# P·V banks as two tiles, and the third score tile given back behind attention for two one-bank tiles

## The chip, the cores and the metric

The kernel runs on one core of a Trainium2 chip. Times are device microseconds (us) of that core. A run's time is the span from the first to the last instruction, plus 1.8 us around it in the profiled execution.

The core has TensorE (PE, with its weight loads shown as PEld), VectorE (DVE), ScalarE (ACT), GpSimd (POOL), and SyncE (SP), which issues the transfers. PE's products go to PSUM, which this kernel uses as eight banks of 128 partitions by 512 fp32 words.

## What is computed

Three layers, all in fp32 values:

```
scores = (mean of neighbouring query pairs) @ k.T / sqrt(64)     # 4 x 8 heads, 576 x 1152
x = softmax(scores) @ v                                          # 2304 tokens x 512
h = x @ w_in ; g = where(h > 0, h, exp(min(h, 0)) - 1)           # 2304 x 2048
x = g @ w_out                                                    # 2304 x 512
logits = x @ phi                                                 # 2304 x 32 slots
d = softmax over tokens ; slots = d.T @ x                        # 32 x 512
slot_out = relu(slots @ w1[e]) @ w2[e]                           # 8 experts
out = softmax over slots(logits) @ slot_out                      # 2304 x 512
```

## The kernel before

**Stages.** Attention runs over 16 pairs of heads. Each pair has 18 steps: two halves `h` of the query columns times nine chunks `c` of 128 keys. A step forms scores of both heads in a score tile (L664), ACT takes the exponential (L676), POOL or DVE adds it to a running sum (L685), and PE multiplies it with V (L671). P·V of half 0 accumulates in PSUM bank `psC[0]`, that of half 1 in `psC[1]`. At the end of a half, ACT copies the result out (L500, the helper of all copies), PE forms the column sums in the same bank (L695) and ACT takes them (L698).

The next pair's keys are prepared during the last steps of a half. PE transposes them (L580), two thirds into a score tile, one third into `psC[1]`, while half 0 of the pair before still accumulates in `psC[0]`. ACT makes the rounded copy (L587), DVE the remainder (L588). Row maxima go through `psC[h]` too (L642, L649).

The dense layer runs over 32 slots (8 groups of weights for three batches together, then 8 for the last). The hidden product (L817) goes to tile `psA`; ACT and DVE apply the ELU (L828 to L831) and split it into two rounded parts (L500, L503). The output product (L856) comes in groups of six products: column half `t = 0` in `psC[0]`, `t = 1` in `psC[1]`. DVE adds each group to X (L867). As each batch ends, the slot layer's first part runs between these groups: logits (L875, L881), transposes (L1019, L969), slot sums (L1023), and weights of the slots (L1042). Its PSUM is `psB[0]` and `psB[1]`, the two banks of the third score tile. The experts (L1180, L1208) read 32 MB of weights, and the last products (L1239) alternate between `psA` and `psB` and are scaled by ACT (L1244) or DVE (L1246).

**PSUM tiles.** There are four tiles of two banks each. `psA` has two; the third of `psT` serves scores during attention (`psS = psT`), and its two halves are `psB`. `psC` is two halves of one tile:

```
psT = [psum.tile([P, 2, 512], F32, name=f"psA{i}") for i in range(3)]
psCt = psum.tile([P, 2, 512], F32, name="psC")
psB = [psT[2][:, i] for i in range(2)]
psC = [psCt[:, i] for i in range(2)]
```

**Order.** `Plan` sets the order. Every operation is recorded with a planned time, its engines, its duration, and what it reads and writes; the plan orders them by a list schedule with engine costs, and emits them by planned start. In the plan's own book, the banks are separate names (`("C", 0)`, `("C", 1)`, `B` in places 4 and 5). The waits between engines are not written by the plan. The layer that holds the tiles adds them when an instruction is emitted, from the tiles that it touches. Each engine runs its queue in order, so a waiting instruction holds what is queued behind it.

Of the kernel before, what the change touches and what calls it, by code (L numbers as in the profile page):

```python
# [8 lines left out]
F32 = mybir.dt.float32  # L9
# [6 lines left out]
PSUM = bass.MemoryType.PSUM  # L16
# [14 lines left out]
def dve(n):  # L31
    return n / 960 + 0.145
# [18 lines left out]
class Plan:  # L51
# [11 lines left out]
    def add(self, t, eng, dur, fn, r=(), w=(), size=0.0, mode="F", port=False, fixed=False):  # L63
        if isinstance(eng, str):
            eng, dur = (eng,), (dur,)
        cls = (self.tag or str(self.phase)) + "".join(x.rstrip("0123456789") for x in w[0][:2] if isinstance(x, str)) + (eng[0] if len(eng) == 1 else "*")
        self.ops.append([t, len(self.ops), eng, dur, fn, r, w, size, BIAS[3 if self.tag else self.phase], t + PRI.get(cls, 0.0), cls, mode, port, fixed])
# [214 lines left out]
def attention_moe_softmoe(  # L282
# [12 lines left out]
    nc = tc.nc  # L295
    P = 128
    B, H, S, D = q.shape
# [4 lines left out]
    NP = B * H // 2  # L302
# [3 lines left out]
    KD = DM // P  # L306
# [7 lines left out]
    PAIR = 2 * NC * STEP  # L314
# [5 lines left out]
    plan = Plan(LOOK)  # L320
    add = plan.add
# [3 lines left out]
    psum = ctx.enter_context(tc.tile_pool(name="psum", bufs=1, space=PSUM))  # L325
# [7 lines left out]
    phi_sb = const.tile([P, KD, 2, NS], F32, name="phi_sb")  # L333
    wscr = dram.tile([2, NG, P, KD * GF * P], F32, name="wscr")
    rscr = [dram.tile([2 * NC, D], F32, name=f"rscr{i}") for i in range(2)]
    psT = [psum.tile([P, 2, 512], F32, name=f"psA{i}") for i in range(3)]
    psCt = psum.tile([P, 2, 512], F32, name="psC")
    psA, psS = psT[:2], psT
    psB = [psT[2][:, i] for i in range(2)]
    psC = [psCt[:, i] for i in range(2)]  # L340
    plan.rot.update(A=[(0, 1), (2, 3)], B=[(4,), (5,)], S=[(0, 1), (2, 3), (4, 5)])
    for name, cnt in (("E", 3), ("U", 3), ("H", 5), ("L", 5)):
        plan.rot[name] = [(f"{name}{i}",) for i in range(cnt)]
# [26 lines left out]
    def carve(kind, name, n, size, off=None, first=0, late=False):  # L370
        lo = top[kind] if off is None else off
        res = []
        for i in range(first, first + n):
            plan.region((name, i), BASE[kind] + lo, BASE[kind] + lo + size)
            res.append(MEM[kind][:, lo : lo + size] if not late else (lambda lo=lo: MEM[kind][:, lo : lo + size]))
            lo += size
        if off is None:
            top[kind] = lo
        assert lo <= SIZE[kind], (kind, name, lo)
        return res  # L380

    def v3(ap, a):
        return ap.rearrange("p (a b) -> p a b", a=a)
# [5 lines left out]
    X = [v3(x, KD) for x in carve("f", "X", B, KD * NQ)]  # L389
# [158 lines left out]
    def T(p, d, x):  # L548
        return (NU * p + 2 * d) * STEP + x
# [207 lines left out]
    def swap(kind, es, name, t, dtype=F32):  # L757
        def go():
            es.close()
            pool = es.enter_context(tc.tile_pool(name=name, bufs=1, side="right" if kind == "y" else "left", reuse_waits="tile"))  # L760
            MEM[kind] = pool.tile([P, SIZE[kind]], dtype, name="mem" + name)

        plan.region((name, 0), BASE[kind], BASE[kind] + SIZE[kind])
        add(t, "SP", 0.0, go, w=[(name, 0)])

    swap("z", z_es, "z", T(NP, -7, 0), F32R)


    plan.phase = 1
# [545 lines left out]
```

## Time and profile before

| | us |
|---|---|
| median of 3 runs | 1062.39 |
| lowest, highest | 1060.51, 1062.91 |
| the profiled execution | 1060.78 |
| its span | 1059.0 |
| attention, about | 16 to 510 |
| dense layer, with slot work in its second half | 510 to 957 |
| rest of the slot layer, experts, output | 957 to 1059 |

PE is busy for 94% of the span, DVE for 65%, POOL for 55%, ACT for 47%. The chain of work that ended last passes through PE for 79% of the span and through DVE for 12%. In a view of the timeline, a row has the start, the duration, the engine, the line, the operation and its tiles, the count of instructions merged in it, and in brackets the idle time of the engine just ahead of it with what ended that. In a view of the waits, a row has the waiting engine and line, what ended the wait, the total, how often, and the longest.

### The profile page before, as it was taken

Reading aid. Unit: us, or ns where it says so; the run is one execution under the profiler, and the core shown is the slowest. Engines: PE = TensorE matmul, PEld = TensorE weight load, DVE = VectorE, ACT = ScalarE, POOL = GpSimd, SP = SyncE. Lnnn points to the kernel's source line nnn. Section 1 sums busy time; section 2 is a strip of 40 time slices with the busy share of each in tenths; the row PEclk is TensorE's granted clock in tenths of the full one; section 3 lists DMA queues with packets and bytes.
Section 4 is the critical chain, followed back from the end, with each engine's and each line's share of the span. In section 5 each row is a group of like instructions: output and inputs, shape, how many; then the busy total and the mean of one; then the engine's idle time right before and its main releaser. Section 6 shows DMA issues by size and latency. Waiting matters only on the chain.

```text
span 1059.0 us, 21663 instructions
## 1 busy us (share of the span) xinstructions
PE 995.6 (94%) x8838; PEld 806.9 (76%) x8838; DVE 691.3 (65%) x1141; ACT 499.6 (47%) x886; POOL 583.9 (55%) x387
## 2 busy tenths in 40 slices
PE   8999999999999999999999999999999999998975
PEld 6677776767766677777799999999999888884322
DVE  4676687888888777779688788775445455444000
ACT  1455555655555555556664434443345464522022
POOL 1678889877888888886734443443235443330000
PEclk8899999999999999999999999999999999998875
DMA  7133324233334432103343334353021213114998
GB/s 162 46 81 68 99 59 122 66 85 110 81 80 109 99 80 58 65 13 108 105 158 115 109 98 130 110 170 119 27 94 41 100 48 112 59 62 140 320 348 285
DMA packets 111827, 114.92 MB, mean 109 GB/s; under 512 B 43632, under 2 KB 83056, under 8 KB 111728
## 3 DMA queue, kind: packets, MB, share of 16 engines
q1 hardware_dynamic: 111728, 113.55, 35.8%
q8 instruction: 69, 1.13, 0.4%
q14 instruction: 30, 0.25, 0.1%
HBM read 100.27 MB, written 13.18 MB: 107 GB/s over the span
## 4 chain that ended last, share of the span: by engine, by line
PE 79%; DVE 12%; ACT 3%; DMA 3%; issue 1%; POOL 1%; SPq 1%; ACTq 0%; DVEq 0%; POOLq 0%
PE psC L856 20%; PE psA L817 18%; PE psA L664 12%; PE psC L671 12%; PE psA L596 5%; DVE memf L605 2%; DVE memf L867 2%; DMA memf<-in_moe_w_dram 2%; ACT memf L676 2%; PE psA L1180 2%; PE psC L695 1%; PE psC L642 1%; PE psC L705 1%; DVE memf L544 1%; PE psA L580 1%
## 5 line engine op out<-in xcount | busy, mean ns | idle before, releaser
L685 POOL TENSOR_TENSOR memf<-memf 128x576 f32<-128x576 f32 x246 | 367.0, 1494 | 77.0 <-ACT memf L676 55.8
L605 DVE TENSOR_REDUCE memf<-psA 128x4 f32<-128x768 f32 (+3 forms) x375 | 240.2, 663 | 75.0 <-ACT memf L676 48.5
L856 PE MATMUL psC<-memr,memz 128*128 128x288 f32 x1512 | 230.6, 300 | 11.7 <-DVE memf L867 8.2
L676 ACT ACTIVATE memf<-psA 128x576 f32<-128x576 f32 x288 | 184.7, 651 | 110.2 <-PE psA L596 85.4
L856 PEld LDWEIGHTS psC<-memr,memz 128*128 128x128 f32 x1512 | 207.6, 189 | 25.0 <-DVE memf L867 19.5
L671 PE MATMUL psC<-memf 128*64 128x288 f32 x1152 | 173.9, 420 | 9.5 <-DVE memr L588 4.4
L503 POOL TENSOR_TENSOR memr<-memf,memr 128x576 fp32r<-128x576 f32 x56 | 85.8, 1536 | 162.8 <-ACT memr L500 141.6
L867 DVE TENSOR_TENSOR memf<-psC,memf 128x288 f32<-128x288 f32 x220 | 93.2, 452 | 121.7 <-PE psC L856 120.7
L817 PE MATMUL psA<-memr,memz 128*128 128x288 f32 x768 | 140.7, 296 | 0.0
L671 PEld LDWEIGHTS psC<-memf 128*64 128x64 f32 x1152 | 68.9, 136 | 61.9 <-issue 8.5
L817 PEld LDWEIGHTS psA<-memr,memz 128*128 128x128 f32 x768 | 115.0, 188 | 0.2
L664 PE MATMUL psA<-memr 64*128 64x288 f32 x1152 | 99.8, 300 | 0.3 <-ACT memf L676 0.3
L664 PEld LDWEIGHTS psA<-memr 64*128 64x128 f32 x1152 | 83.8, 185 | 12.5 <-issue 6.7
L828 ACT ACTIVATE memf<-psA 128x576 f32<-128x576 f32 x64 | 41.7, 651 | 103.4 <-PE psA L817 101.2
L500 ACT CAST memr<-memf 128x576 fp32r<-128x576 f32 x87 | 57.4, 674 | 68.5 <-DVE memf L831 63.1
L664 PE MATMUL psA<-memy 64*128 64x288 f32 x864 | 86.5, 305 | 0.4 <-DVE memf L605 0.4
L503 POOL TENSOR_TENSOR memz<-memf,memz 128x1024 fp32r<-128x1024 f32 x22 | 53.4, 2428 | 52.1 <-ACT memz L500 44.4
L817 PE MATMUL psA<-memr,memv 128*128 128x288 f32 x384 | 78.2, 296 | 0.0
L664 PEld LDWEIGHTS psA<-memy 64*128 64x128 f32 x864 | 66.2, 187 | 9.9 <-issue 4.3
L817 PEld LDWEIGHTS psA<-memr,memv 128*128 128x128 f32 x384 | 61.8, 189 | 1.1 <-issue 0.9
L596 PE MATMUL psA<-memy 64*128 64x384 f32 (+3 forms) x366 | 57.6, 317 | 3.7 <-DVE memf L605 2.7
L831 DVE SCALAR_TENSOR_TENSOR memf<-memf,psA 128x576 f32<-128x576 f32 x64 | 47.7, 745 | 13.1 <-ACT memf L829 13.0
(173 smaller groups left out, 1319.0 us busy)
## 6 DMA issues: line engine op xcount, KB each, us to landing
memf<-in_moe_w_dram SPq DMA_DIRECT2D x38, 512.0 KB
memf<-wscr SPq DMA_DIRECT2D x32, 512.0 KB
memz<-in_q_dram SPq DMA_DIRECT2D x32, 288.0 KB
memz<-in_k_dram SPq DMA_DIRECT2D x32, 288.0 KB
memf<-in_v_dram SPq DMA_DIRECT2D x16, 576.0 KB
memf<-in_moe_w_in_dram SPq DMA_DIRECT2D x32, 256.0 KB
wscr<-memf SPq DMA_DIRECT2D x32, 256.0 KB
memf<-in_moe_w_out_dram SPq DMA_DIRECT2D x16, 512.0 KB
```

The lines of the kernel that those rows point to most:

```text
L500: return lambda e: nc.scalar.copy(out_, in_) if e == "ACT" else nc.vector.tensor_copy(out_, in_)
L503: return lambda e: ENG[e].tensor_tensor(out_, a, b, ALU.subtract)
L596: nc.tensor.matmul(tile_[:m, j, lo : lo + n * MW], lhsT=qkb["qh", i][js, o : o + m], rhs=qkb["kh", i][js, g * MW : (g + n) * MW], start=Tr ...
L605: add(t, "DVE", dve(2 * n * MW), lambda: nc.vector.reduce_max(MX[i][:m, a, :, g : g + n], v4(got(psS, tok)[:m, :, lo : lo + n * MW], n), a ...
L664: nc.tensor.matmul(sp[:, j, :NH], lhsT=qkb[w, i][js, cs] if w else ONER[js], rhs=qkb[m, i][js, hs], start=(x == 0), stop=(x == 3))
L671: nc.tensor.matmul(psC[h][j * D : (j + 1) * D, :NH], lhsT=VR[i][:, j, c], rhs=e[:, j], start=(c == 0), stop=(c == NC - 1))
L676: add(t + 0.01, "ACT", act(NQ, True), lambda: nc.scalar.activation(got(EAf, E_), got(psS, S_)[:, :, :NH], AF.Exp, scale=1.0 / 16.0), r=[S_ ...
L685: ENG[e].tensor_tensor(ac, a, got(EAf, E_), ALU.add)
L817: nc.tensor.matmul(ph[:, t, :NH], lhsT=a, rhs=x, start=(i == 0), stop=(i == 3 * KD - 1))
L831: add(t + 1.2, "DVE", dve(NQ), lambda: nc.vector.scalar_tensor_tensor(got(Ef, uk), got(Uf, ek), -1.0, ph(), ALU.add, ALU.max), r=[ek, A], ...
L856: nc.tensor.matmul(po_(), lhsT=a, rhs=x, start=(i == 0), stop=(i == 3 * GF - 1))
L867: add(t0 + 0.8, "DVE", dve(NH), lambda: nc.vector.tensor_tensor(d, po_(), d, ALU.add), r=[ck], w=XK)
```

## The change

The two banks of `psC` become two tiles of one bank. The third two-bank tile stays in a PSUM pool of its own; once the last attention result has been written, the plan closes that pool and opens another in its place with two one-bank tiles `psB`. Two DVE memsets, one for each new tile, are added to the plan. Nothing is computed differently.

```diff
-    psT = [psum.tile([P, 2, 512], F32, name=f"psA{i}") for i in range(3)]
-    psCt = psum.tile([P, 2, 512], F32, name="psC")
-    psA, psS = psT[:2], psT
-    psB = [psT[2][:, i] for i in range(2)]
-    psC = [psCt[:, i] for i in range(2)]
+    psA = [psum.tile([P, 2, 512], F32, name=f"psA{i}") for i in range(2)]
+    psC = [psum.tile([P, 512], F32, name=f"psC{i}") for i in range(2)]
+    ps_es = ctx.enter_context(ExitStack())
+    psS = psA + [ps_es.enter_context(tc.tile_pool(name="psum3", bufs=1, space=PSUM)).tile([P, 2, 512], F32, name="psS2")]
+    psB = []
...
+    def swap_ps():
+        ps_es.close()
+        pool = ps_es.enter_context(tc.tile_pool(name="psumB", bufs=1, space=PSUM, reuse_waits="tile"))
+        psB.extend(pool.tile([P, 512], F32, name=f"psB{i}") for i in range(2))
+
+    plan.region(("psS2", 0), 500000, 500001)
+    plan.region(("psB", 0), 500000, 500001)
+    add(NP * PAIR + 60, "SP", 0.0, swap_ps, r=[("X", B - 1, KD - 1, 0), ("X", B - 1, KD - 1, 1)], w=[("psB", 0)])
+    for i in range(2):
+        add(NP * PAIR + 64, "DVE", dve(512), lambda i=i: nc.vector.memset(psB[i], 0.0), r=[("psB", 0)], w=[("pb0", i)])
```

PE keeps all its 7,786 instructions in the same order, and so does SP. On DVE, ACT and POOL, the order differs only in one stretch of the dense layer around the memsets. What differs elsewhere is which instructions wait, and for what. The rows below give the queue's instructions with what they wait for in brackets, as semaphores of an engine (`DVE_49` is DVE's) or of a transfer queue (`DMAHW`).

PE at the end of a pair of attention, before; the first four rows multiply with V, and L695 forms the sums of the half that has ended:

```order
L664 MATMUL psA_80<-memy,memr 128x288 x2
L596 MATMUL psA_80<-memy 64x192 x2
L671 MATMUL psC<-memf 64x288 [waits DMAHW4_49,Activation_49]
L671 MATMUL psC<-memf 64x288
L671 MATMUL psC<-memf 64x288 [waits DVE_49]
L671 MATMUL psC<-memf 64x288
L695 MATMUL psC<-memf 64x288 [waits Pool_49]
```

The same place now; `psC_80` and `psC_81` are the two new tiles, `psS_85` the third score tile:

```order
L596 MATMUL psS_85<-memy 64x192 x2
L671 MATMUL psC_80<-memf 64x288 [waits DMAHW4_49]
L671 MATMUL psC_80<-memf 64x288 x3
L695 MATMUL psC_81<-memf 64x288 [waits DVE_49,Pool_49]
L695 MATMUL psC_81<-memf 64x288
L664 MATMUL psA_79<-memy 128x288 x6
```

The wait for DVE has moved from the second product with V to the sums. On DVE, in the same place, the remainder of the keys that stands in `psC` before:

```order
L588 TENSOR_TENSOR memr<-psA_79,memr 128x768 [waits Activation_49]
L588 TENSOR_TENSOR memr<-psC,memr 128x384 [waits PE_49,Activation_49]
L605 TENSOR_REDUCE memf<-psA_78 64x2 [waits Activation_49]
L605 TENSOR_REDUCE memf<-psA_80 64x2 [waits Activation_49]
L646 TENSOR_REDUCE memf<-memf 128x4 [waits DVE_49]
```

and now:

```order
L588 TENSOR_TENSOR memr<-psA_79,memr 128x768 [waits Activation_49]
L588 TENSOR_TENSOR memr<-psC_81,memr 128x384 [waits Activation_49]
L605 TENSOR_REDUCE memf<-psA_78 64x2 [waits Activation_49]
L605 TENSOR_REDUCE memf<-psS_85 64x2 [waits Activation_49]
L646 TENSOR_REDUCE memf<-memf 128x4 [waits DVE_49]
```

Its wait for PE is gone. In the dense layer, PE's output products before; twelve are two groups of six, one for each bank:

```order
L817 MATMUL psA_78<-memr,memz 128x288 x12
L856 MATMUL psC<-memr,memz 128x288 [waits DVE_49]
L856 MATMUL psC<-memr,memz 128x288 x11
L817 MATMUL psA_78<-memr,memz 128x288 x12
L856 MATMUL psC<-memr,memz 128x288 [waits DVE_49]
```

and now (L828 and L867 are L817 and L856 of before, eleven lines further down):

```order
L828 MATMUL psA_78<-memr,memz 128x288 x12
L867 MATMUL psC_81<-memr,memz 128x288 [waits DVE_49]
L867 MATMUL psC_81<-memr,memz 128x288 x5
L867 MATMUL psC_80<-memr,memz 128x288 [waits DVE_49]
L867 MATMUL psC_80<-memr,memz 128x288 x5
```

Each group of six now has a wait of its own. On DVE, each add now waits for PE itself (L878 is L867 of before); before, only the first of two had a wait:

```order
L878 TENSOR_TENSOR memf<-psC_81,memf 128x288 [waits PE_49]
L503 TENSOR_TENSOR memr<-memf,memr 128x576 [waits Activation_49]
L878 TENSOR_TENSOR memf<-psC_80,memf 128x288 [waits PE_49]
L492 SCALAR_TENSOR_TENSOR memf<-memf 128x512 [waits Pool_49]
L485 SCALAR_TENSOR_TENSOR memf<-memf 128x512
```

In all, PE's instructions wait for 1,166 semaphores instead of 1,050, and DVE's for 1,214 instead of 1,137. The two memsets stand in DVE's queue between steps of the weight decoding (L480 to L489) and have no wait.

## Rows read from the trace of the kernel before

**Rows 1.** Stretches: start and end, length, busy us by engine, PEclk, DMA, GB/s.
```profile
16.00:510.00 494.00, 474.57 (x5058) 346.49 (x5056) 388.15 (x569) 270.12 (x464) 396.93 (x268) 0.99 0.30 80
553.00:800.00 247.00, 244.08 (x1813) 240.62 (x1812) 170.53 (x315) 102.26 (x150) 100.61 (x61) 1.00 0.33 108
```

**Rows 2.** Timeline at the end of one pair of attention.
```profile
93.49 0.49 ACT L587 CAST memr<-psC 128x384 fp32r<-128x384 f32 x1
...
93.62 0.96 DVE L588 TENSOR_TENSOR memr<-psA,memr 128x768 fp32r<-128x768 f32 x1 [0.61 <-ACT memr L587]
...
94.46 0.71 PE L671 MATMUL psC<-memf 128*64 128x288 f32 x4
...
95.28 0.56 DVE L588 TENSOR_TENSOR memr<-psC,memr 128x384 fp32r<-128x384 f32 x1 [0.70 <-ACT memf L676]
...
95.90 0.20 PEld L671 LDWEIGHTS psC<-memf 128*64 128x64 f32 x4 [1.24 <-DVE memr L588]
...
96.19 0.39 PEld L695 LDWEIGHTS psC<-memf 128*64 128x64 f32 x4
```

**Rows 3.** Waits of PE's weight loads in attention: total us, times, longest.
```profile
PEld psC L671 <- issue: 8.5, 50, 0.2
PEld psC L671 <- DVE memr L588: 7.4, 6, 1.2
PEld psC L671 <- DVE memy L588: 7.4, 6, 1.2
```

**Rows 4.** Waits of DVE in attention.
```profile
DVE memr L588 <- PE psC L671: 1.5, 2, 1.2
...
DVE memy L588 <- PE psC L671: 0.5, 1, 0.5
```

**Rows 5.** Waits of PE's weight loads from 553 to 957 us.
```profile
PEld psC L856 <- DVE memf L867: 19.5, 44, 1.4
PEld psA L1042 <- DVE memr L1029: 1.7, 1, 1.7
```

**Rows 6.** Timeline of DVE and of PE's loads at two places in the dense layer.
```profile
608.03 2.65 DVE L483 TENSOR_SCALAR memf<-memf 128x512 int32<-128x512 int32 x1
...
612.14 0.96 PEld L856 LDWEIGHTS psC<-memr,memz 128*128 128x128 f32 x7 [1.43 <-DVE memf L867]
...
636.50 0.46 DVE L867 TENSOR_TENSOR memf<-psC,memf 128x288 f32<-128x288 f32 x1 [1.37 <-PE psC L856]
...
637.54 0.45 DVE L867 TENSOR_TENSOR memf<-psC,memf 128x288 f32<-128x288 f32 x1
...
638.04 1.62 PEld L856 LDWEIGHTS psC<-memr,memz 128*128 128x128 f32 x12 [0.23 <-DVE memf L867]
```

**Rows 7.** Timeline of PE in the last slot, and in the slot layer behind it; one of DVE.
```profile
946.97 1.06 PE L856 MATMUL psC<-memr,memz 128*128 128x288 f32 x6 [0.55 <-DVE memf L867]
...
961.57 1.18 PE L875 MATMUL psA<-memf,phi_sb 128*64 128x288 f32 x4 [1.03 <-ACT memf L500]
...
975.63 1.60 PE L1264 MATMUL psA<-slot_sum,memf 64*128 64x32 f32 x8 [0.52 <-ACT memr L500]
...
977.74 0.29 DVE L1267 COPY memf<-psA 128x128 f32<-128x128 f32 x1 [2.97 <-PE psA L1042]
```

**Rows 8.** What SP's queue waited for from 880 us on, longest.
```profile
SPq L1165 <- PE psA L1180: 26.0, 10, 18.0
```

**Rows 9.** A stretch of the experts, columns as in the first group.
```profile
1020.00:1030.00 10.00, 8.84 (x76) 4.74 (x75) 2.40 (x4) 5.07 (x13) 0.00 (x0) 0.81 1.10 349
```

**Rows 10.** Timeline of the last products and their scaling.
```profile
1045.77 2.07 PE L1239 MATMUL psA<-memr 96*128 96x256 f32 x8 [0.91 <-DVE memr L1223]
...
1047.45 2.29 ACT L1244 ACTIVATE memf<-psA,memf 128x256 f32<-128x256 f32 x6 [2.19 <-PE psA L1239]
...
1048.32 0.69 DVE L1246 TENSOR_TENSOR memf<-psA,memf 128x512 f32<-128x512 f32 x1 [2.61 <-ACT memf L1244]
1049.06 1.65 PE L1239 MATMUL psA<-memr 96*128 96x256 f32 x6 [1.23 <-DVE memf L1246]
```

## The prediction

> **What bounds the kernel now.** I read the table of stretches first. In attention PE is busy for 474.6 of 494 us, in the first half of the dense layer for 244.1 of 247 us; DVE has 388.2 and 170.5 us of work there, POOL 396.9 and 100.6 [rows 1]. So PE sets the pace up to 957 us, and what makes PE wait is worth time. Next I read the waits of PE's weight loads, since the load shows a stop that a pipelined product hides. Two kinds stand out, and in both PE waits for DVE at `psC`: L671 for L588, 14.8 us in 12 waits [rows 3], and L856 for L867, 19.5 us in 44 waits [rows 5]. Last I read the timeline at such places, to see whether the wait is needed.
>
> It mostly isn't. At the end of a pair of attention [rows 2], PE multiplies with V into `psC[0]` at 94.46 (0.71 us, so until 95.17). DVE's second L588 reads the new keys from `psC[1]`. Its input is there since ACT's L587 ended at 93.98, and DVE is free from 94.58 on, yet L588 starts at 95.28, 0.11 us behind the end of L671. The page puts that wait down to ACT's L676, which ended at 95.27, but L588 waits for PE and for the copy L587 in the program. Then the next L671, again into `psC[0]`, waits until L588 has ended at 95.84. Each waits for the other although they use different banks. The old tile covers both banks, and the waits are made for the tile.
>
> The dense layer shows the same [rows 6]. L867 for the first group starts at 636.50, after 1.37 us of idle time that PE ended, and the second add ends at 637.99; PE's next group starts at 638.04, behind the second add, though it writes the bank that the first had emptied at 636.96.
>
> **The change part by part.** The sum is made against the profiled execution, 1060.8 us, which is 1.6 us under the median of the runs.
>
> *Attention.* With two tiles, L588 follows its predecessor at 94.58 and ends at 95.14. The second L671 needs nothing, so it goes 0.29 us behind the first (the distance from 95.90 to 96.19), at 94.75, and the sums L695 could go at 95.04 [rows 2]. They do write `psC[1]` and take over the wait for L588, so they start about 0.05 us behind its end, at 95.2 instead of 96.19. The 1.24 us wait of the load thus gives 1.0 us: twelve times [rows 3], 12.0 us. Three more pair ends have the idle time on DVE, 2.0 us in all, named as waiting for L671 [rows 4]; there L695 starts earlier by that time: 2.0 us. Together 14.0. The bounds are 8 (if PE's gain is half used up before the pair ends) and 17 (all load idle).
>
> *Dense layer.* An add can now start when its own group of six ends, which is 0.8 us sooner for the first (twelve loads take 1.62 us), and the next group on that bank waits for it alone. At 638.04 the whole 0.23 us goes [rows 6]. Of the 19.5 us [rows 5], two parts stay. In the waits where a group follows the add of its own bank, as at 946.97 with 0.55 us of PE idle [rows 7], nothing changes: I count eight of those in the timeline, about 4 us. Where DVE itself is late, as behind the L483 that took 2.65 us at 608.03, a part of the wait (1.43 us at 612.14) remains [rows 6]: two such places, about 1.5 us left. That gives 19.5 - 4 - 1.5 = 14.0 us, between 7 (half) and 18.
>
> *Banks of the slot layer (`psB`).* A transpose L1042 waits 1.7 us for a subtraction L1029 that reads the other bank [rows 5]: 1.7 us, between 0 and 1.7, since the copies beside it may be late next. Behind the dense layer, the second half of the logits, L875, waits 1.03 us for ACT's copy of the first half from the other bank; L1264 waits 0.52 us for a copy of the other bank; and the copy L1267 starts at 977.74, behind L1042, though L1264, whose result it reads, ended at 977.23, 0.5 us before [rows 7]. These lie in one chain: 2.0 us, between 1 and 2.5.
>
> *The experts* follow whatever comes before them. SP's longest wait there, 18.0 us, is for PE's L1180 [rows 8], and from then on the transfers run at 349 GB/s with all 16 DMA engines busy (a share of 1.10) [rows 9]. A chain that reaches L1180 earlier therefore ends earlier by as much.
>
> *The last products* [rows 10]. PE issues eight L1239 from 1045.77 on, in 2.07 us, for four tiles; ACT's first scaling starts only at 1047.45, behind the third tile, which is in the other `psB` bank, and DVE's at 1048.32, behind ACT. PE then waits 1.23 us for DVE before 1049.06. The first tile is done a quarter of 2.07 us on, with the latency near 1046.5, so ACT can start 0.9 us sooner, and DVE needs only PE. The 1.23 us of PE goes: 1.2 us, between 0.9 and 2.
>
> *What is added.* Two memsets of 512 columns on DVE, between steps of the decoding. The trace has none into PSUM; the nearest rows are an add of 288 columns there, 0.45 us, and the 512-column L483, held up to 2.65 us [rows 6]. I take 0.6 us each, near the first, 1.2 us. DVE has 76 us without work in the 247 us behind them [rows 1], so they cost nothing; without that cover 1.2 us, at most 5.3. The plan's changed order around them moves one split of weights from DVE to POOL; POOL has even more room. The swap of the pools issues no instruction.
>
> The sum is 14.0 + 14.0 + 1.7 + 2.0 + 1.2 = 32.9 us. 1060.8 - 32.9 = 1027.9; on the scale of the medians 1029.5. I forecast 1029 us. With all lower bounds the gain is 17, with all upper ones 41.
>
> The waits become finer, so there are more of them and more signals: some 110 first groups of the pairs now signal by themselves. The Trainium skill (TensorE: Matmul & The Clock Gate, "The cost: per-tile semaphore tail") gives 26.3 ns for each increment in a row. By that, an estimate is 110 x 0.026 = 2.9 us, and the sum would be 30.0 us. No row here shows a price of a signal by itself.
>
> **The rivals.**
>
> *Another engine takes PE's place.* Where PE no longer stops, it runs into DVE's own queue or a true dependence a step later. For it: POOL has work for 397 of 494 us in attention and DVE for 388 [rows 1], and the 2.65 us of L483 shows that DVE can be held up for long [rows 6]. Against it: DVE gets freer too, since its idle time before L588 and L867 goes. If half of the 28 us in attention and dense layer come back as other waits, the gain is 19 and the time 1043; with the lower bounds elsewhere, 1046.
>
> *The change does nothing.* The Trainium skill (Perfetto Trace Analysis, "Matmuls") says that groups rotating through different PSUM banks let the emptying of one overlap the products of the next; the kernel before already rotates. If the banks overlapped already, what I see would be waits for other things, and the time would stay at 1062. Against it speak the 0.11 us between the end of L671 and L588 and the L671 that follows only behind L588 [rows 2]; here the trace differs from the rule.
>
> *Slower, by finer waits.* PE's and DVE's instructions wait for 193 semaphores more. In attention, 50 loads of L671 show 8.5 us of "issue", 0.17 us each [rows 3], at instructions with more than one wait. If each new wait cost that in the open, 33 us would be lost, as much as is gained; it decides from 0.17 us on, and at 0.3 us each the time would be 1062 - 33 + 58 = 1087. Against it: the load is idle then, but the products before it still run, so PE's own busy time has no hole.
>
> **How the numbers follow.** The forecast, waits gone and most of it PE's to keep: 0.77, with 1020 to 1037 as its own range, which holds partial losses of about 8 us and, on the other side, more of the bounds. Another engine takes over: 0.16, 1038 to 1052. Nothing: 0.04, 1062. Slower: 0.03, 1087. The range of 1020 to 1042 holds the forecast and some of the first rival, and leaves out about 0.2. A measurement of this kernel can tell about 0.2%, 2 us, from no change. Faster: 0.77 + 0.16 = 0.93; the same 0.04; slower 0.03.
>
> **What would show it.** In the profile after, the waits of L671 for L588 should be gone and L695 should wait for it at most 0.2 us a time; L588 should follow its predecessor; the waits at the output products should fall from 19.5 to about 6 us; the start of L1180 should come near 947 instead of 978 us; and ACT's first scaling should start about 0.8 us behind PE's first L1239 instead of 1.7. If attention still ends near 510 us, the first step is wrong. If PE's waits are gone but new ones for L605, L676 or the splits L503 stand in their place, the first rival holds. If `psC` waits stay, the tile was not the cause.

## The result and the profile after

| | before | after |
|---|---|---|
| median of 6 runs each, us | 1061.45 | 1020.67 |
| lowest, highest | 1059.16, 1063.02 | 1018.34, 1021.48 |
| span of the profiled execution | 1059.0 | 1017.7 |
| ratio | | 0.9614 (0.9597 to 0.9632) |

The kernel is 3.9% faster. The time lies inside the forecast's range of 1020 to 1042, at its lower end: 41 us were gained where 32.9 had been worked out, and 41 is also what all its upper bounds together give.

The page of the kernel after: busy time of the engines, the chain that ended last by engine, and one group each of PE's products with V and of DVE's adds (behind the last bar: idle time before them and what ended it).

```profile
PE 979.6 (96%) x8838; PEld 806.5 (79%) x8838; DVE 690.6 (68%) x1141; ACT 498.4 (49%) x886; POOL 591.7 (58%) x389
...
PE 84%; DVE 8%; DMA 3%; ACT 2%; issue 1%; SPq 0%; ACTq 0%; POOL 0%; DVEq 0%; POOLq 0%
...
L671 PE MATMUL psC<-memf 128*64 128x288 f32 x1152 | 171.3, 419 | 0.0
...
L878 DVE TENSOR_TENSOR memf<-psC,memf 128x288 f32<-128x288 f32 x220 | 99.3, 459 | 96.1 <-PE psC L867 94.8
```

DVE's share of the chain has gone from 12% to 8%. The two stretches of [rows 1], cut at the same instructions of PE (start and end, length, busy us by engine, PEclk, DMA, GB/s):

```profile
15.40:495.60 480.20, 470.75 (x5058) 347.25 (x5056) 381.41 (x569) 270.13 (x465) 399.46 (x268) 0.99 0.32 82
537.70:777.80 240.10, 240.10 (x1813) 240.10 (x1812) 170.10 (x312) 101.37 (x149) 104.52 (x63) 1.00 0.35 110
```

Attention's 494 us have become 480.2, and PE stands for 9.5 of them instead of 19.4. The first half of the dense layer took 247 us and now takes 240.1, in which PE has no hole left. A pair's end in attention, the place of [rows 2] (start, duration, engine, line, idle time before it in brackets):

```profile
91.08 0.96 DVE L588 TENSOR_TENSOR memr<-psA,memr 128x768 fp32r<-128x768 f32 x1 [0.60 <-ACT memr L587]
...
91.91 0.68 PEld L671 LDWEIGHTS psC<-memf 128*64 128x64 f32 x8 [0.17 <-issue]
...
91.95 0.55 DVE L588 TENSOR_TENSOR memr<-psC,memr 128x384 fp32r<-128x384 f32 x1
...
92.69 0.39 PEld L695 LDWEIGHTS psC<-memf 128*64 128x64 f32 x4
```

The second L588 follows the first, beside PE's products, and all eight loads of L671 go in one row. From the first L671 to the first L695 it is 0.78 us; before, it was 1.73 (94.46 to 96.19 [rows 2]).

**Where the gain lies.** PE runs the same instructions in the same order in all kernels here, so the start of each can be compared between two traces. The table gives the gain over the kernel before, in us, that PE's starts win within a stretch (named by the starts in the trace of before), for the kernel after and for the seven experiments below. The last stretch is from PE's last weight load to the end of the span.

| stretch | after | e1 | e2 | e3 | e4 | e5 | e6 | e7 |
|---|---|---|---|---|---|---|---|---|
| head, to 24 | 0.6 | 0.1 | -0.3 | 0.1 | -0.4 | 0.1 | 0.1 | 1.1 |
| attention, 24 to 505 | 13.7 | 13.5 | 0.1 | 14.0 | 0.1 | 11.2 | 5.9 | 0.2 |
| 505 to 553 | 1.0 | 1.0 | -0.1 | -1.0 | -1.0 | 0.2 | 1.8 | 1.4 |
| dense, 553 to 957 | 21.6 | 18.3 | 2.2 | 0.0 | 19.0 | 14.7 | 14.0 | 2.0 |
| chain behind it, 957 to 978 | 2.4 | -1.0 | 3.9 | -0.9 | -0.1 | 2.5 | 2.2 | 3.9 |
| experts, 978 to 1046 | 0.9 | 0.0 | -0.3 | 0.1 | -0.1 | -0.1 | 0.0 | 0.6 |
| last products, to 1051 | 2.0 | 0.0 | 2.0 | 0.0 | 0.0 | 2.0 | 2.0 | 2.0 |
| to the end | -0.8 | 0.0 | -0.7 | 0.0 | 0.0 | -0.7 | -0.7 | -0.8 |
| span | 41.3 | 31.8 | 6.6 | 12.2 | 17.6 | 29.7 | 25.2 | 10.3 |

The head is the same work in all of them and still differs by some 1.4 us between e4 and e7, in the hundred products L705 that `warm` puts at the kernel's start. So 0.6 us of the 41.3 isn't the change's.

### The profile page after: what moved, and what is told of

Read it like the earlier page. It is cut to its first block, busy times and chain, and to the rows that moved or that the text cites. A ratio compares the mean times of both kernels' runs of the same rounds, so it can differ in the third digit from the quotient of the medians.

```text
span 1017.7 us, 21700 instructions
## 1 busy us (share of the span) xinstructions
PE 979.6 (96%) x8838; PEld 806.5 (79%) x8838; DVE 690.6 (68%) x1141; ACT 498.4 (49%) x886; POOL 591.7 (58%) x389
## 4 chain that ended last, share of the span: by engine, by line
PE 84%; DVE 8%; DMA 3%; ACT 2%; issue 1%; SPq 0%; ACTq 0%; POOL 0%; DVEq 0%; POOLq 0%
PE psA L828 20%; PE psC L867 19%; PE psC L671 13%; PE psA L664 9%; PE psS L664 5%; PE psA L596 3%; DVE memf L605 2%; DMA memf<-in_moe_w_dram 2%; PE psS L596 2%; PE psA L1191 2%; PE psC L695 1%; PE psC L642 1%; PE psC L705 1%; ACT memf L676 1%; DVE memf L544 1%
## 5 line engine op out<-in xcount | busy, mean ns | idle before, releaser
L867 PE MATMUL psC<-memr,memz 128*128 128x288 f32 x1512 | 225.3, 297 | 2.4 <-ACT memf L500 2.3
L867 PEld LDWEIGHTS psC<-memr,memz 128*128 128x128 f32 x1512 | 207.9, 189 | 6.0 <-ACT memf L500 3.4
L605 DVE TENSOR_REDUCE memf<-psA 128x2 f32<-128x384 f32 (+3 forms) x248 | 161.7, 665 | 50.1 <-ACT memf L676 32.9
L671 PE MATMUL psC<-memf 128*64 128x288 f32 x1152 | 171.3, 419 | 0.0
L503 POOL TENSOR_TENSOR memr<-memf,memr 128x576 fp32r<-128x576 f32 x57 | 87.4, 1537 | 139.8 <-ACT memr L500 120.7
L878 DVE TENSOR_TENSOR memf<-psC,memf 128x288 f32<-128x288 f32 x220 | 99.3, 459 | 96.1 <-PE psC L867 94.8
L676 ACT ACTIVATE memf<-psA 128x576 f32<-128x576 f32 x190 | 122.9, 651 | 78.5 <-PE psA L596 61.2
L828 PE MATMUL psA<-memr,memz 128*128 128x288 f32 x768 | 140.7, 296 | 0.0
L828 PEld LDWEIGHTS psA<-memr,memz 128*128 128x128 f32 x768 | 114.9, 188 | 0.2
L671 PEld LDWEIGHTS psC<-memf 128*64 128x64 f32 x1152 | 69.9, 136 | 48.6 <-issue 8.9
L605 DVE TENSOR_REDUCE memf<-psS 128x2 f32<-128x384 f32 (+3 forms) x127 | 84.0, 661 | 27.2 <-ACT memf L676 17.8
L839 ACT ACTIVATE memf<-psA 128x576 f32<-128x576 f32 x64 | 41.7, 651 | 121.5 <-PE psA L828 120.5
L503 POOL TENSOR_TENSOR memz<-memf,memz 128x1024 fp32r<-128x1024 f32 x23 | 56.4, 2452 | 49.9 <-ACT memz L500 49.9
L676 ACT ACTIVATE memf<-psS 128x576 f32<-128x576 f32 x98 | 63.8, 651 | 35.4 <-PE psS L596 30.1
L828 PE MATMUL psA<-memr,memv 128*128 128x288 f32 x384 | 78.2, 296 | 0.0
L664 PE MATMUL psA<-memr 64*128 64x288 f32 x744 | 66.3, 300 | 0.6 <-ACT memf L676 0.3
L828 PEld LDWEIGHTS psA<-memr,memv 128*128 128x128 f32 x384 | 61.7, 188 | 0.8 <-issue 0.4
L664 PEld LDWEIGHTS psA<-memr 64*128 64x128 f32 x744 | 54.4, 185 | 8.3 <-issue 4.4
L664 PE MATMUL psA<-memy 64*128 64x288 f32 x582 | 58.2, 305 | 0.0
```

Of the source, the lines that this page charges most:

```text
L503: return lambda e: ENG[e].tensor_tensor(out_, a, b, ALU.subtract)
L605: add(t, "DVE", dve(2 * n * MW), lambda: nc.vector.reduce_max(MX[i][:m, a, :, g : g + n], v4(got(psS, tok)[:m, :, lo : lo + n * MW], n), a ...
L664: nc.tensor.matmul(sp[:, j, :NH], lhsT=qkb[w, i][js, cs] if w else ONER[js], rhs=qkb[m, i][js, hs], start=(x == 0), stop=(x == 3))
L671: nc.tensor.matmul(psC[h][j * D : (j + 1) * D, :NH], lhsT=VR[i][:, j, c], rhs=e[:, j], start=(c == 0), stop=(c == NC - 1))
L676: add(t + 0.01, "ACT", act(NQ, True), lambda: nc.scalar.activation(got(EAf, E_), got(psS, S_)[:, :, :NH], AF.Exp, scale=1.0 / 16.0), r=[S_ ...
L828: nc.tensor.matmul(ph[:, t, :NH], lhsT=a, rhs=x, start=(i == 0), stop=(i == 3 * KD - 1))
```

## Experiments: the parts by themselves

The theory: the waits of [rows 3 to 7] are made by the two-bank tiles, each part of the change takes away its own, and the parts add up. The rivals shift the gain between the parts, or give some of it back later. Each ratio below is to runs of the kernel before that were made beside the experiment (median 1059.64 us for e1 to e4, 1063.38 us for e5 to e7). A gain of e1 to e4 in us is that ratio applied to 1059.64 us; the difference of the medians alone is 1.1 to 2.5 us smaller, as the kernel before scatters there from 1057.87 to 1064.60 us.

**e1, `psC` alone.**

```diff
-    psCt = psum.tile([P, 2, 512], F32, name="psC")
+    psC = [psum.tile([P, 512], F32, name=f"psC{i}") for i in range(2)]
...
-    psC = [psCt[:, i] for i in range(2)]
```

> Only psC becomes two tiles; psB stays the two halves of the third score tile, and there is no swap and no memset. Theory (each part takes away its own waits, and the parts add up; the psB part is worth what the waits at psB were, some 6 us of the 41 us): gain 34 to 36 us against before, 1026 us. Rival (the dense layer gained more than I had forecast because slot work on psB stands between the groups on PE, so psB carries some 8 us more): gain 27 us, 1034 us. If the psB tiles did nothing: 1020.5 us.

Measured: 1027.37 us, ratio 0.9685 (0.9664 to 0.9706), a gain of 33.4 us. That fits the theory (34 to 36, within the interval) and not the rival's 27: `psC` carries four fifths. Within this kernel the waits at `psB` come out plainly. Waits of PE's loads from 538 to 925 us of e1 (L855, L866 and L1041 are L856, L867 and L1042 of before):

```profile
PEld psA L1041 <- DVE memr L1028: 1.7, 1, 1.7
PEld psC L855 <- DVE memf L866: 1.4, 4, 0.4
PEld psA L1041 <- ACT memr L499: 0.6, 1, 0.6
```

The 44 waits of 19.5 us [rows 5] are down to four of 1.4 us. Behind L1041, e1 shows a lower clock all through 831 to 833 us, of which the last section tells (columns as above):

```profile
831.00:833.00 2.00, 2.00 (x11) 2.00 (x10) 1.97 (x3) 1.74 (x3) 2.00 (x2) 0.50 0.02 4
833.00:835.00 2.00, 2.00 (x16) 2.00 (x16) 0.83 (x2) 0.64 (x4) 1.33 (x1) 0.94 0.69 256
```

**e2, `psB` alone.** The swap and the memsets as in the kernel after, with `psC` as before:

```diff
-    psC = [psum.tile([P, 512], F32, name=f"psC{i}") for i in range(2)]
+    psCt = psum.tile([P, 2, 512], F32, name="psC")
+    psC = [psCt[:, i] for i in range(2)]
```

> Only the third score tile is swapped for two one-bank tiles psB, with the two memsets; psC stays one tile of two banks. Theory: gain about 6 us (1.7 at the slot weights, 2.4 in the chain behind the dense layer, 2 at the last products), 1055 us, with no gain ahead of 800 us of the span. Rival (psB carries the excess of the dense layer's second half): gain 13 us, 1048 us. If the memsets cost in the open, 1.2 us of loss at about 590 us shows in the times at which PE's instructions start.

Measured: 1053.91 us, ratio 0.9933 (0.9915 to 0.9950), a gain of 7.1 us. The size fits the theory, and the rival's 13 us is outside the interval. e1 and e2 together gain 3.15% + 0.67% = 3.82%; the whole change gains 3.86%. The parts add up within the intervals of some 0.2% each. By the spans in the table they give 38.4 of the 41.3 us; some 1 us each is missing in the dense layer, where e1's clock fell (last section), at the experts and at the head. The memsets took 0.485 us each, at 537 and 539 us of e2, and the stretch from 505 to 553 us loses only 0.1 us. One thing was expected otherwise, no gain ahead of 800 us: behind the memsets e2 gains 1.4 us from 553 to 590 us, at three waits of L856 on `psC`. In that stretch the order on DVE, ACT and POOL has changed with the memsets.

**e3 and e4, `psC` by stages.** e3 has two tiles through attention and the first slot, then one; e4 the reverse. At the change the pool is closed and opened again, and `psC` is refilled, with two memsets on DVE (shown for e3; e4 takes two tiles of one bank):

```diff
+    def swap_c(done=[]):
+        if done:
+            return
+        done.append(1)
+        c_es.close()
+        pool = c_es.enter_context(tc.tile_pool(name="psumD", bufs=1, space=PSUM, reuse_waits="tile"))
+        t = pool.tile([P, 2, 512], F32, name="psCd")
+        psC[:] = [t[:, i] for i in range(2)]
+        for x in psC:
+            nc.vector.memset(x, 0.0)
...
         def mm():
+            if n == 1:
+                swap_c()
```

In both, the swap stands between the last product group of the first slot and the copy that reads it, so this one group of products is lost to the memset and is missing in the output; all the work is done.

> psC is two tiles during attention and the first slot of the dense layer, then one tile of two banks (with two memsets on DVE at the change); psB as before. Theory: attention's 15 us stay, since everything behind follows PE: 1046.5 us, and from 560 us on PE's instructions keep a constant distance to those of before. Rival (the stops of PE in attention gave DVE and POOL time that they need later, so that part of the gain is given back in the dense layer): gain 8 to 11 us, 1051 to 1053 us.

> psC is one tile of two banks during attention and the first slot of the dense layer, then two tiles (with two memsets on DVE at the change); psB as before. Theory: gain 19 to 21 us, nearly the whole of the 19.5 us of waits at the output products, since a group that follows the add of its own bank finds that add done earlier too: 1041 us. Rival (my forecast: the eight waits at the own bank and two late places of DVE stay, and the rest of the 21 us comes from psB): gain 14 us, 1047 us.

Measured: e3 1048.44 us, ratio 0.9871 (0.9849 to 0.9893), 13.7 us; e4 1042.50 us, ratio 0.9824 (0.9802 to 0.9847), 18.6 us. Together 3.05%, beside 3.15% of e1. In e3 attention gains 14.0 us, and through the whole dense layer PE keeps that distance (0.0): nothing of it is given back, so the rival of e3 falls. In e4 the dense layer gains 19.0 us, more than my forecast for it; the rival of e4 (14) lies below its trace, and with 18.6 - 2.4 = 16.2 below the interval too. The 1.0 us that both lose from 505 to 553 us comes of the swap: the first product group behind it starts 1.8 us (e3, which had gained 0.8 us ahead of it) and 1.1 us (e4) later than it would.

## Experiments: which of the two waits

A wait stands on both sides: PE's product waits for the reader of the other bank, and the reader waits for the product into the other bank. These three are the kernel after, with one side or both written in again by hand. Nothing is computed in addition, and each engine's order stays. `also` makes an instruction wait for another one; for each bank, `wrote` holds the last product into it and `took` its last reader on each engine:

```diff
+            ks = {k[1] for k in (*ops[i][5], *ops[i][6]) if k[0] == "C"}
+            if ks:
+                new = self.tc.nc.cur_bb.bb.instructions[n0:]
+                k = ks.pop()
+                if where[i] == "PE":
+                    for e in ("ACT", "DVE"):
+                        if PE_SIDE and (1 - k, e) in took:
+                            self.also(new[0], took[1 - k, e])
+                    wrote[k] = new[-1]
+                else:
+                    if READ_SIDE and 1 - k in wrote:
+                        self.also(new[0], wrote[1 - k])
+                    took[k, where[i]] = new[-1]
```

**e7, both sides.**

> The kernel after, with its two psC tiles, but with the waits of one tile written in by hand on both sides: a product into one bank also waits for the last reader of the other bank, and a reader of one bank also waits for the last product into the other. No instruction is added. Theory (the whole gain of psC is these waits; the banks and the order play no part): the time of the run with psB alone, 1054 us, 0.993 of before. Rival (part of the gain comes from elsewhere, the changed place of the tiles or the order around the swap): 1040 us or less.

Measured: 1053.60 us, ratio 0.9913 (0.9899 to 0.9928); e2, which has one `psC` tile, had 0.9933 (0.9915 to 0.9950). With the waits back, the gain of `psC` is gone, to a few tenths of a per cent, though its tiles stay apart. So the theory holds, and the rival's 1040 us falls: it is the waits, and not the place of the tiles. Guarding by a pair of banks costs 3.0% here (0.9913 against 0.9614). The Trainium skill (PSUM — Partial Sum Buffer, "Summary: rules for kernel authors") asks for semaphores by the bank where PSUM is read while products run into it.

**e5, PE's side.**

> As the kernel after, but PE's products into one psC bank also wait for the last reader of the other bank; the readers wait for their own bank alone. Theory (the two waits make a circle, each reader being held back by PE first and PE then by the reader; with one of them gone the reader starts 0.7 to 0.8 us earlier and is done when PE comes): attention loses 0.3 to 0.4 us at each of 12 to 15 pair ends, some 5 us, and the dense layer 2 to 6 us; 1030 us (1027 to 1032). Rival (PE's own waits are all that counts, since PE sets the pace): the whole psC part of 33 us is lost, 1054 us.

**e6, the reader's side.**

> As the kernel after, but a reader of one psC bank (DVE's adds and remainders, ACT's copies) also waits for the last product into the other bank; PE waits for the own bank alone. Theory: at a pair end of attention L588 starts 0.7 us late and the column sums wait for it, 0.5 to 0.7 us at 15 pair ends, some 9 us; in the dense layer an add of the first group is 0.8 us late and a group that follows on its own bank waits, 4 to 9 us; 1035 us (1031 to 1040). Rival (PE's own waits are all that counts): DVE's later start is hidden, 1021 to 1023 us.

Measured: e5 1032.58 us, ratio 0.9718 (0.9701 to 0.9735), so 1.04% or 11 us worse than the kernel after; e6 1035.38 us, ratio 0.9746 (0.9730 to 0.9762), 1.32% or 14 us worse. e6 came out as expected, e5 just above its 1027 to 1032 us. Neither of the rivals (all of it on PE's side, nothing on the other) holds. The two sides lose 2.36% one by one and 2.99% together: in a circle, taking either wait away also shortens the other.

The same pair's end in e5 (21 lines further down: L692, L609 and L716 are L671, L588 and L695):

```profile
93.00 0.55 DVE L609 TENSOR_TENSOR memr<-psC,memr 128x384 fp32r<-128x384 f32 x1
93.60 0.20 PEld L692 LDWEIGHTS psC<-memf 128*64 128x64 f32 x4 [0.44 <-DVE memr L609]
```

and in e6:

```profile
93.95 0.56 DVE L609 TENSOR_TENSOR memr<-psC,memr 128x384 fp32r<-128x384 f32 x1 [0.70 <-ACT memf L697]
94.63 0.23 PEld L716 LDWEIGHTS psC<-memf 128*64 128x64 f32 x4 [0.82 <-issue]
```

In e5 DVE goes at once and PE waits 0.44 us; twelve such ends lose 2.5 us in the table, half of what I had expected. In e6 DVE waits its 0.70 us again, and the column sums, which need it, follow 0.8 us late: 7.8 us in attention, near the expected 9. There the reader's side is the dearer. In the dense layer both cost about the same, 7.0 us in e5 (I had expected 2 to 6) and 7.7 us in e6. The waits of PE's loads there in e5 (L888 and L899 are L856 and L867; total, times, longest):

```profile
PEld psC L888 <- DVE memf L899: 8.0, 20, 0.7
```

in e6:

```profile
PEld psC L888 <- DVE memf L899: 7.8, 17, 0.8
```

and in e7:

```profile
PEld psC L888 <- DVE memf L899: 18.5, 41, 1.4
```

Both sides together bring back 41 waits of 18.5 us, nearly the 44 of 19.5 us [rows 5].

## Why the prediction was right, and where it was too small

*Attention: right.* Forecast 14.0 us, measured 13.7 (after), 13.5 (e1), 14.0 (e3). The waits of L671 for L588 [rows 3] are gone. One sign came out worse than I had said: L695 was to wait for L588 at most 0.2 us, but at two pair ends, where the first L588 itself is late, its load stands 0.97 and 0.66 us. The profile names no releaser for the load, but L588 for the product:

```profile
205.03 0.54 DVE L588 TENSOR_TENSOR memr<-psC,memr 128x384 fp32r<-128x384 f32 x1
...
205.68 0.23 PEld L695 LDWEIGHTS psC<-memf 128*64 128x64 f32 x4 [0.97 <-issue]
205.72 0.71 PE L695 MATMUL psC<-memf 128*64 128x288 f32 x4 [0.49 <-DVE memr L588]
```

Otherwise no new wait has taken the place of the old ones, as the first rival had it. In the trace of before, the loads of L596 waited for the row maxima L605 like this in attention:

```profile
PEld psA L596 <- DVE memf L605: 20.3, 42, 1.1
```

In that of after they do so in two rows, since the third score tile has a name of its own now:

```profile
PEld psA L596 <- DVE memf L605: 13.7, 29, 0.7
...
PEld psS L596 <- DVE memf L605: 6.8, 13, 1.1
```

42 waits of 20.3 us before, 42 of 20.5 after. That the change does nothing fell with the result. The rival "slower, by finer waits" fell as well: the "issue" of L671 [rows 3], on which it stood, is 8.7 us in 51 waits after and hardly differs in any run, however many semaphores are waited for. The estimate of 2.9 us from the Trainium skill (TensorE: Matmul & The Clock Gate, "The cost: per-tile semaphore tail") is about signals in the dense layer. There 272 of the output products signal in the kernel after and 178 in that before, PE has no hole in the first half, and the gain is larger than worked out, not smaller: a price of the signals does not show. Nor does one of the waits' number: e7 waits for fewer semaphores than the kernel after (PE for 1,074 and DVE for 1,131, against 1,166 and 1,214) and is 3.0% slower.

*The dense layer: the failed step.* The prediction said that of the 19.5 us "two parts stay", 4 us at groups that follow the add of their own bank and 1.5 us where DVE is late. In the kernel after, 1.1 us stay, in four waits. The last slot, where [rows 7] has such a wait at 946.97, now looks like this:

```profile
910.24 3.24 PEld L867 LDWEIGHTS psC<-memr,memz 128*128 128x128 f32 x24 [0.24 <-DVE memf L878]
910.25 3.47 PE L867 MATMUL psC<-memr,memz 128*128 128x288 f32 x24
911.34 0.46 DVE L878 TENSOR_TENSOR memf<-psC,memf 128x288 f32<-128x288 f32 x1 [0.79 <-PE psC L867]
912.14 0.46 DVE L878 TENSOR_TENSOR memf<-psC,memf 128x288 f32<-128x288 f32 x1 [0.34 <-PE psC L867]
```

Four groups go without a stop. The wait for the own bank's add was needed, but the add came late only since it waited for the next group of PE first. Before, it started at 946.46, behind the twelve products that began at 944.57; now at 911.34, 1.09 us behind the first of them, while the second group runs. I had counted what PE waits for and not asked what the awaited add had waited for. e6 shows it by experiment: there PE waits for its own bank alone, the adds start late as before, and 7.8 us in 17 waits stay, more than the 5.5 us that I had called unavoidable. So the two sides had to go together.

The 1.5 us of the late DVE went as well. The places of [rows 6] in the timeline of after (DVE and PE's loads; the first two rows are one place, the last two the other):

```profile
590.24 0.42 DVE L483 TENSOR_SCALAR memf<-memf 128x512 int32<-128x512 int32 x1
...
593.39 0.72 PEld L867 LDWEIGHTS psC<-memr,memz 128*128 128x128 f32 x5
...
616.80 0.46 DVE L878 TENSOR_TENSOR memf<-psC,memf 128x288 f32<-128x288 f32 x1 [1.27 <-PE psC L867]
...
618.85 0.32 PEld L867 LDWEIGHTS psC<-memr,memz 128*128 128x128 f32 x2
```

The load that stood 1.43 us at 612.14 doesn't wait, and L483 takes 0.42 us instead of 2.65 (the last section says why). But a late DVE need not stop PE any more either. L487 was late before, and PE's load stood 0.49 us behind it:

```profile
647.70 2.14 DVE L487 TENSOR_SCALAR memf<-memf 128x512 int32<-128x512 int32 x1
...
651.29 0.83 PEld L856 LDWEIGHTS psC<-memr,memz 128*128 128x128 f32 x6 [0.49 <-DVE memf L867]
```

After, it is as late, and the load doesn't wait:

```profile
628.16 2.50 DVE L487 TENSOR_SCALAR memf<-memf 128x512 int32<-128x512 int32 x1
...
631.58 0.58 PEld L867 LDWEIGHTS psC<-memr,memz 128*128 128x128 f32 x4
```

So `psC` is worth 19.0 us here (e4), not 14.0. A further 1.0 us came from 505 to 553 us, a stretch that my rows on waits left out. The 19.0 us lie above the upper bound of 18 too. The time stayed inside the range because attention stayed 3 us below its own upper bound of 17 and so made room for this; that part is luck.

*`psB`: sizes about right, clock not foreseen.* In the dense layer, the transposes L1042 gained 1.4 us in e2 at the place that I had put at 1.7; e2's other gains there are the 1.4 us by the changed order, less a later loss of 0.7 us. In the chain of 957 to 978 us I had 2.0; the kernel after gained 2.4, and e2 3.9, of which a part is the clock (below). *The last products*: forecast 1.2 us. ACT's first scaling starts 0.89 us behind PE's first product (1.68 before), and DVE's 1.69 us behind it (L1250, L1255 and L1257 are L1239, L1244 and L1246 of before):

```profile
1005.66 0.80 PE L1250 MATMUL psB<-memr 96*128 96x256 f32 x2 [0.92 <-DVE memr L1234]
...
1006.55 0.84 ACT L1255 ACTIVATE memf<-psB,memf 128x256 f32<-128x256 f32 x2 [1.39 <-PE psB L1250]
...
1007.35 0.69 DVE L1257 TENSOR_TENSOR memf<-psB,memf 128x512 f32<-128x512 f32 x1 [1.74 <-PE psB L1250]
```

PE's last loads gain 2.0 us, but the way from them to the end takes 0.8 us more: 1.2 us at the end.

*The experts* follow 1:1, as forecast: L1180 (L1191 in the kernel after) starts at 938.83 instead of 978.09, 39.3 us earlier, and the last products begin 40.1 us earlier.

By the sum: the forecast was 32.9, the trace has 41.3. The 8.4 us between them are 5.94 in the dense layer from 553 us on (4.4 of them the waits that were to stay, 5.5 less 1.1; the rest is `psB` there, with the clock and the changed order), 0.99 from 505 to 553, 0.85 at the experts, 0.58 at the head and 0.37 in the chain, less 0.33 in attention. No run here beats the kernel after, and what waits remain at `psC` in the dense layer, 1.1 us, are too few for another step of this kind.

## What to carry to other kernels

Look in the trace for an engine that starts just behind another engine's work on a neighbouring PSUM bank, and give each bank that is filled and emptied by itself a tile of its own; the order of instructions need not change for it. When two engines wait for each other, don't count the remaining wait of one with the other's start held fixed: ask first when the awaited work could have begun. And a wait removed here can be priced by putting it back by hand on one side at a time.

## What the runs showed of the hardware

**TensorE's clock fell behind the same waits in one run and not in another.** In e1, PE stood for 0.35 and 1.55 us at the transposes of the slot weights, and the granted clock was 0.50, the lower of the two levels (1.2 GHz), from 831 to 833 us. In the kernel before, PE stood there for the same 0.35 and 1.55 us, and the clock stayed at 1.00. Against it, PE's starts in e1 fell back by 1.5 us there. The kernel before:

```profile
854.00:856.00 2.00, 2.00 (x15) 1.93 (x16) 0.77 (x2) 1.83 (x5) 1.78 (x1) 1.00 0.01 4
```

The chain behind the dense layer shows it too. A stretch of it before:

```profile
969.00:972.00 3.00, 3.00 (x11) 1.90 (x10) 0.99 (x3) 2.04 (x9) 0.00 (x0) 0.53 0.36 130
```

and in e2:

```profile
966.00:969.00 3.00, 2.50 (x13) 1.35 (x12) 1.79 (x5) 2.77 (x13) 0.00 (x0) 1.00 0.81 305
```

e2 kept 1.00 up to the experts and gained 3.9 us in the chain; the kernel after fell to 0.54 from 931 to 934 us and gained 2.4; e1 and e3, which change nothing there, lost 1.0 and 0.9, with stretches of 3 us at 0.66 and 0.50 in e1 and at 0.55 and 0.69 in e3. Why the clock fell in one run and not in another stayed open. So two runs with the same change in the chain, e2 and the kernel after, differ there by 1.5 us, and that part isn't steady.

**A short DVE instruction took six times as long beside POOL.** In the trace of before, POOL began a subtraction just ahead of the L483 of [rows 6], which started at 608.03:

```profile
608.00 2.40 POOL L503 TENSOR_TENSOR memz<-memf,memv 128x1024 fp32r<-128x1024 f32 x1 [3.25 <-ACT memv L500]
```

L483 ended at 610.68, 0.28 us after POOL. In the kernel after, L483 went first, at 590.24, and took 0.42 us; POOL's subtraction followed at 590.55. The Trainium skill (SBUF — State Buffer, "Who interferes with whom") says that the two engines share a pair of ports: where DVE runs in a mode with two ports, which a `tensor_scalar` like L483 can enter, the first of the two engines holds the pair for its whole instruction while the other stands. The trace agrees, with 2.65 us against 0.42.

Which engine went first hung on the waits at `psC`. At this place POOL started 0.02 to 0.04 us ahead, and the instruction of L483 took 2.65 or 2.66 us, in all five kernels whose readers wait for the other bank too (before, e2, e3, e6, e7). In the four others (after, e1, e4, e5) it started 0.31 us ahead of POOL and took 0.42 us. In e6 (L504 and L524 are L483 and L503):

```profile
598.34 2.40 POOL L524 TENSOR_TENSOR memz<-memf,memv 128x1024 fp32r<-128x1024 f32 x1 [3.26 <-ACT memv L521]
598.36 2.66 DVE L504 TENSOR_SCALAR memf<-memf 128x512 int32<-128x512 int32 x1
```

So a shift of some 0.3 us by a false wait came back as 2.2 us on DVE, since it let the other engine go first.
